# Another hand-written order for a fused attention and channel-mix kernel: other steps of VectorE and GpSimd lie beside each other, and early gaps of TensorE take more zero matmuls

## The chip, the core and the metric

One core of a Trainium2 chip runs the program. The metric is the device time of one launch in microseconds (us). The engines are TensorE (PE in the profile; PEld for its weight loads), VectorE (DVE), ScalarE (ACT), GpSimd (POOL) and SyncE (SP), which issues most of the DMAs. Each engine does its instructions in the order in which the program hands them over; semaphores hold an instruction until its inputs are there and its output buffer is free.

## The reference

Inputs: q, k, v of 4 batches x 4 heads x 1088 positions x 32, two sketches S1, S2 of 8 x 32, and the weights of a channel mix of width 128 with 1024 hidden units.

```python
def phi(x):
    a = np.einsum('rd,bhsd->bhsr', S1, x)
    b = np.einsum('rd,bhsd->bhsr', S2, x)
    return np.einsum('bhsi,bhsj->bhsij', a, b).reshape(*x.shape[:-1], r * r)
q_p, k_p = (phi(q), phi(k))
kv = np.einsum('bhsf,bhsd->bhfd', k_p, v)
z = np.sum(k_p, axis=2)
num = np.einsum('bhsf,bhfd->bhsd', q_p, kv)
den = np.einsum('bhsf,bhf->bhs', q_p, z)[..., None] + 1e-06
x = num / den            # heads side by side: 4 x 1088 x 128
x_prev = x one position earlier, zeros first
xk = mu_k * x + (1.0 - mu_k) * x_prev
xr = mu_r * x + (1.0 - mu_r) * x_prev
k = np.maximum(xk @ w_k, 0.0)
out = 1.0 / (1.0 + np.exp(-(xr @ w_r))) * (k * k @ w_v)
```

## The kernel before

The program is a list of small tasks, written out by hand in a table `ORDER` and carried out in that order; the kernel's last loop looks each name up and calls the function of that name. Nothing else decides the order: an engine's queue is the sequence of the table's entries that use the engine. An entry reads `name.batch.part.engine@banks`. The engine's letter is V (VectorE), A (ScalarE), G (GpSimd) or P (VectorE, with one factor read straight from PSUM); the digits behind @ are PSUM banks that the entry writes.

For each of the 4 batches (first number b):
- `turn.k`, `turn.q` (L259, L262) transpose k and q in 32 x 32 blocks on VectorE; `kproj` (L272, L278) multiplies with the sketches, `abev` (L200) copies the result out of PSUM.
- `kp` (L296) forms phi(k): products of two sketch values, each factor repeated 8 times by a step of zero in its access pattern. The first part of a batch has 1280 elements a partition, the second 1024. `kvmm` (L325), `kvev`, `kvt`, `kvtev` make the summary kv and turn it; `zmm`, `zev`, `wmm`, `wsq` make z and place it in the matrix `SQ`.
- `abw` (matmuls L359, L363, L375, L382) and `abwev` project q; `pw` (L403), `den` (L410, L411) and `an` (L419) form the denominator and scale one factor with it, repeating it; `qp` (L428) forms the scaled phi(q) with repeated factors, parts of 1152 and 1024 elements.
- For batch 0 `qt`/`qtt`, `qtev`/`qttev` transpose qp by TensorE; for the others `qd` (L437) does it on VectorE. `xmm` (L489, L506) and `xt` (L469, L475) give x in PSUM, `xev` and `xtev` copy it to `qx`, `xs` copies the 31 boundary values of a partition to where the shifted x needs them.

Then, for 9 groups g of up to 512 columns (two per batch, the ninth of 256 columns over all batches): `xk`, `xkt` (L522, L525) mix x with its shift, `xh` and `xht` cast x to bf16 (544 or 96 elements), `f1` (L546) multiplies with w_k in four parts, `relu` (L554, ScalarE) empties PSUM, `sq` (L567 on ScalarE, L569 elsewhere) squares, `f2` (L579) multiplies with w_v, `rr` (L592) with w_r, `sig` (L600) is the sigmoid, `fin` (L605) multiplies the two and issues four stores (L612).

`cset`, `smm` and `wset` prepare constants and weights; `wset.0` scales and casts w_k to bf16 (L208, 1024 elements). `zz.n` issues n matmuls of zeros (L173) that nothing reads. Every copy and cast goes through one helper, so L202 stands for all of VectorE's and GpSimd's and L200 for ScalarE's.

```python
def zz(n, banks):
    for i in range(n):
        nc.tensor.matmul(PS[:, banks[0], :], zero[:, :P], zero[:], skip_group_check=True)

def qp(b, g, eng):                                   # L421
    ...
    b_ = pslot(b, g, 0) if eng == "P" else x[:, s0:s1, 0]
    e = nc.gpsimd if eng == "G" else nc.vector
    e.tensor_mul(o[:, :s1 - s0], _ap(a_, list(a_.ap[1:]) + [[0, R]]),
                 _ap(b_, [list(b_.ap[1]), [0, R], list(b_.ap[2])]))

for entry in ORDER.split():                          # L617
    ...
    does[name](*args)
```

Of the kernel before, what the change touches and what calls it, by code (L numbers as in the profile page):

```python
# [35 lines left out]
turn.q.0.1.V kproj.0.1@1 turn.q.0.0.V abev.0.1.A zz.2@7 zmm.0@2 zev.0.V zz.1@7 wmm.0 wsq.0 zz.1@7 abw.0.0@1
abwev.0.0.A kp.0.0.P kp.0.1.G abw.0.1@2 abwev.0.1.A pw.0.0.V den.0.0 an.0.0.G turn.k.1.2.V qp.0.0.P kvmm.0@0 kvev.0.A
pw.0.1.G den.0.1 zz.1@7 kvt.0 zz.1@7 kproj.1.0@3 abev.1.0.A kproj.1.1@4 abev.1.1.A qtt.0@3 qt.0.0@56 qttev.0.A
kvtev.0.V zmm.1@0 zev.1.A an.0.1.G xt.0 qp.0.1.P cset.3 qtev.0.0.A xtev.0.A turn.q.1.2.V qt.0.1@12 wmm.1 wsq.1
wset.0.G qtev.0.1.A xmm.0.0@7 xev.0.0.A xs.0.V xh.0.0.A kp.1.0.G kp.1.1.P xk.0.0 turn.k.2.2.V wset.2.G abw.1.0@0  # L40
abwev.1.0.A abw.1.1@4 abwev.1.1.A pw.1.2.G den.1.2 f1.0.0@12 relu.0.0.A f1.0.3@56 xmm.0.1@4 wset.1.G relu.0.3.A
kproj.2.1@1 an.1.2.V kproj.2.0@5 sq.0.0.A abev.2.1.A sq.0.3.A xev.0.1.V f1.0.1@67 xk.0.1 abev.2.0.V qp.1.0.G qp.1.1.G
xkt.0 turn.k.3.2.V qd.1.0.V relu.0.1.A f1.1.1@01 zmm.2@5 kp.2.0.G zev.2.A sq.0.1.A f1.1.0@23 relu.1.0.A f1.1.2@67
relu.1.2.A wmm.2 wsq.2 kvmm.1@4 kvev.1.A kproj.3.0@5 f1.0.2@23 kproj.3.1@6 turn.q.2.2.V abw.2.0@7 abev.3.0.V
relu.1.1.A qd.1.1.V abev.3.1.A zmm.3@0 turn.q.3.2.V relu.0.2.A zev.3.A abwev.2.0.A abw.2.1@1 abwev.2.1.V sq.1.2.A
kvt.1 wmm.3 wsq.3 kp.2.1.G kvtev.1.A f1.1.3@23 relu.1.3.A abw.3.0@0 abwev.3.0.A kp.3.1.P xt.1@4 kvmm.2@6 xtev.1.A
xht.0.V sq.0.2.V sq.1.3.A kvev.2.A pw.2.2.G den.2.2 xh.0.1.G xmm.1.2@0123 xev.1.0.A an.2.2.G abw.3.1@7 kvt.2 kp.3.0.P
xs.1.G xev.1.1.A qp.2.0.G qp.2.1.G sq.1.0.A abwev.3.1.V xk.1.0 xk.1.1 xh.1.0.V f2.0.0@5 f2.0.1 sq.1.1.A xkt.1 rr.0@7
sig.0.A f2.0.2 f1.3.3@01 f2.0.3 kvtev.2.V pw.3.2.G relu.3.3.A fin.0.S f1.2.2@23 relu.2.2.A rr.1@6 f1.2.3@01 relu.2.3.A
f1.2.0@45 relu.2.0.A sq.3.3.G sig.1.A kvmm.3@2 qd.2.0.V qd.2.1.V f1.3.1@01 kvev.3.V den.3.2 relu.3.1.A rr.2@3 sig.2.A  # L50
xh.1.1.V kvt.3 xmm.2.2@4567 kvtev.3.V xev.2.0.A xt.2@0 xtev.2.V f2.1.0@1 f2.1.1 xs.2.V xev.2.1.V xk.2.0 an.3.2.G xkt.2
sq.2.0.A xh.2.0.A xk.2.1 f1.2.1@23 relu.2.1.A sq.2.3.V f2.1.2 f2.1.3 rr.3@0 sig.3.A f1.3.0@45 relu.3.0.A f1.5.1@67
sq.2.2.V sq.2.1.V f1.3.2@23 relu.3.2.A f2.2.0@0 relu.5.1.A f2.2.1 f2.2.2 sq.3.1.V f1.4.0@45 qp.3.0.G relu.4.0.A
sq.3.0.V f2.3.0@2 f1.4.2@67 relu.4.2.A sq.3.2.V fin.1.S f2.3.1 f1.4.3@34 relu.4.3.A qp.3.1.G f2.2.3 xh.2.1.V f1.5.0@56
relu.5.0.A qd.3.0.V f2.3.2 f1.4.1@34 fin.2.S rr.4@7 qd.3.1.V relu.4.1.A f2.3.3 fin.3.S f1.5.2@01 xmm.3.2@3456 sig.4.A
sq.4.0.V sq.4.2.V sq.5.1.G relu.5.2.A xev.3.1.A sq.4.1.V xev.3.0.V xt.3@7 f1.5.3@01 f2.4.0@2 f2.4.1 f2.4.2 xtev.3.A
xs.3.G xkt.3 rr.5@7 relu.5.3.A xk.3.0 xk.3.1 f1.6.0@01 sq.5.0.V sq.4.3.A f2.4.3 f1.7.1@34 xht.1.G xht.2.G fin.4.S
f2.5.0@5 sq.5.2.V sq.5.3.V sig.5.A relu.6.0.A relu.7.1.A sq.7.1.V f1.6.1@67 relu.6.1.A xht.3.V f2.5.1 f1.6.2@01
sq.6.0.V f1.8.0@23 sq.6.1.V relu.6.2.A relu.8.0.A sq.8.0.V sq.6.2.V f2.5.2 f1.6.3@67 f2.5.3 fin.5.S relu.6.3.A
# [594 lines left out]
```

## Time and profile before

| | |
|---|---|
| time, median of 3 runs | 87.34 us (86.89 to 91.38) |
| the profiled execution | 86.8 us, of which its span 85.0 us |
| busy, share of the span | TensorE 86%, VectorE 81%, ScalarE 70%, GpSimd 46% |
| chain that ended last, by engine | TensorE 31%, VectorE 21%, DMA 19%, issue 19%, GpSimd 2% |
| granted TensorE clock | 0.987 of full speed over the span |
| bytes read and written | 7.80 MB and 2.23 MB |

The span is what the profiler saw between the first and the last instruction; the remaining 1.8 us lie around it. A row of the timeline gives the start in us from the span's start, the duration, the engine, the source line, the operation and its tiles. A row of groups gives count, busy us and the mean ns of one, then the idle time of the engine ahead of them and what ended it.

### The profile page before, as it was taken

The page shows a single profiled execution, that of the slowest core. Times are in us where ns is not written, and L with a number is a line of the kernel's source. Part 1 is how long each engine was busy: PE and PEld are TensorE (multiplying, and loading weights), DVE is VectorE, ACT ScalarE, POOL GpSimd, SP SyncE. Part 2 cuts the span into 40 slices and gives each one's busy share as a digit, 9 for nine tenths or more (in the row PEclk, how much of TensorE's full clock was granted, in tenths as well). Part 3 has the DMA queues.
Part 4 walks back from the last instruction along what each step waited for, and adds up shares of the span by engine and source line. Part 5 has one row for each costly group of instructions (what it writes and reads, how often), then busy time and mean ns, then how long its engine had stood idle before and what let it go on. Part 6 is the DMA issues. An engine that isn't in the chain of part 4 may idle for free.

```text
span 85.0 us, 3444 instructions
## 1 busy us (share of the span) xinstructions
PE 73.0 (86%) x1471; PEld 54.8 (64%) x1483; DVE 69.2 (81%) x121; ACT 59.6 (70%) x88; POOL 39.4 (46%) x53
## 2 busy tenths in 40 slices
PE   4999798998699998999799996999967999999400
PEld 1368696983447667676676784587836877799300
DVE  5367659899979999795889959999998999989600
ACT  0603041468599999994979988799938999999100
POOL 5050904599188999439978199108001700000110
PEclk9999999999999999999999999999999999999995
DMA  0999999999995200000002200001233313042350
GB/s 1 296 314 253 340 384 243 286 400 410 334 217 147 71 12 0 8 0 12 0 8 59 70 2 8 0 0 47 76 93 79 87 27 100 4 121 65 92 142 17
DMA packets 10131, 10.25 MB, mean 121 GB/s; under 512 B 1170, under 2 KB 7540, under 8 KB 10116
## 3 DMA queue, kind: packets, MB, share of 16 engines
q1 hardware_dynamic: 10016, 9.97, 39.9%
q8 instruction: 11, 0.18, 0.8%
q10 hardware_dynamic: 68, 0.03, 0.2%
q14 instruction: 4, 0.03, 0.2%
q0 software_dynamic: 32, 0.03, 0.1%
HBM read 7.80 MB, written 2.23 MB: 118 GB/s over the span
## 4 chain that ended last, share of the span: by engine, by line
PE 31%; DVE 21%; DMA 19%; issue 19%; POOL 2%; SPq 2%; POOLq 1%; ACT 1%; ACTq 0%; DVEq 0%
DMA qx<-in_q_dram 11%; DMA k<-in_k_dram 7%; PE ps L546 6%; DVE k L569 5%; PE ps L382 5%; PE ps L325 4%; DVE qx L202 4%; PE ps L506 3%; DVE qpT L437 3%; PE ps L272 3%; PE ps L579 2%; DVE k L605 2%; DVE x L202 2%; PE ps L592 2%; PE ps L278 2%
## 5 line engine op out<-in xcount | busy, mean ns | idle before, releaser
L554 ACT ACTIVATE k<-ps 128x1024 bf16<-128x1024 f32 (+1 forms) x36 | 33.0, 996 | 2.1 <-DVE k L569 1.5
L579 PE MATMUL ps<-wv,k 128*128 128x128 bf16 x272 | 19.4, 219 | 0.7 <-issue 0.6
L579 PEld LDWEIGHTS <-k 128*128 128x128 bf16 x272 | 16.8, 98 | 4.4 <-issue 0.7
L546 PE MATMUL ps<-xk,wk 128*128 128x512 bf16 x54 | 16.1, 379 | 0.9 <-ACT k L554 0.4
L569 DVE TENSOR_TENSOR k<-k 128x1024 bf16<-128x1024 bf16 (+1 forms) x25 | 14.8, 641 | 0.3 <-ACT k L554 0.2
L428 POOL TENSOR_TENSOR qp<-an,abw 128x1152 f32<-128x1152 f32 (+1 forms) x6 | 12.3, 2070 | 0.6 <-DVE an L419 0.6
L296 POOL TENSOR_TENSOR kp<-ab 128x1024 f32<-128x1024 f32 (+1 forms) x4 | 8.7, 2176 | 1.9 <-ACT ab L200 1.9
L567 ACT ACTIVATE k<-k 128x1024 bf16<-128x1024 bf16 x9 | 9.5, 1070 | 0.0
L546 PEld LDWEIGHTS <-wk 128*128 128x128 bf16 x72 | 6.0, 99 | 3.0 <-issue 0.6
L437 DVE STREAM_TRANSPOSE qpT<-qp 128x1152 f32<-128x1152 f32 (+1 forms) x6 | 7.6, 1285 | 0.0
L272 PEld LDWEIGHTS ps<-SK,kT 128*128 128x128 f32 x54 | 6.3, 192 | 1.3 <-ACT k L554 0.8
L200 ACT COPY ab<-ps 128x256 f32<-128x256 f32 (+1 forms) x6 | 2.4, 394 | 6.6 <-DVE qT L262 3.8
L612 POOL DMA_DIRECT2D out_dram<-rt x1 | 0.7, 709 | 13.0 <-DVE rt L605 13.0
L382 PE MATMUL ps<-SQ,qT 128*32 128x96 f32 x192 | 5.5, 248 | 1.4 <-DVE kp L296 1.0
L173 PE MATMUL ps<-zero 128*128 128x512 bf16 x15 | 5.6, 487 | 1.2 <-DVE warm L155 1.2
L272 PE MATMUL ps<-SK,kT 128*128 128x64 f32 x54 | 6.6, 276 | 0.0
L262 DVE STREAM_TRANSPOSE qT<-qx 128x1088 f32<-128x1088 f32 (+2 forms) x5 | 5.3, 1069 | 1.1 <-DMA qx<-in_q_dram 1.1
L605 DVE TENSOR_TENSOR k<-ps,k 128x512 f32<-128x512 f32 x8 | 5.4, 677 | 0.9 <-ACT k L554 0.4
L200 ACT COPY abw<-ps 128x432 f32<-128x432 f32 (+1 forms) x6 | 3.1, 516 | 4.1 <-PE ps L363 2.8
L569 POOL TENSOR_TENSOR k<-k 128x1024 bf16<-128x1024 bf16 x2 | 3.8, 1892 | 4.8 <-DVE k L569 3.9
L419 POOL TENSOR_TENSOR an<-abw,den 128x272 f32<-128x272 f32 (+2 forms) x4 | 2.2, 559 | 7.8 <-DVE den L411 7.8
L522 DVE SCALAR_TENSOR_TENSOR xk<-ps,rat,qx 128x512 bf16<-128x512 f32 x8 | 5.8, 740 | 0.0
(106 smaller groups left out, 126.3 us busy)
## 6 DMA issues: line engine op xcount, KB each, us to landing
out_dram<-k SPq DMA_DIRECT2D x32, 64.0 KB, 1.7
k<-in_k_dram SPq DMA_DIRECT2D x6, 272.0 KB, 6.6
qx<-in_q_dram SPq DMA_DIRECT2D x6, 272.0 KB, 6.2
v<-in_v_dram SPq DMA_DIRECT2D x8, 144.0 KB, 6.3
v<-in_v_dram SPq DMA_DIRECT2D x8, 128.0 KB, 4.5
wk_f<-in_moe_w_k_dram SPq DMA_DIRECT2D x1, 512.0 KB
wv_f<-in_moe_w_v_dram SPq DMA_DIRECT2D x1, 512.0 KB, 7.7
k<-in_k_dram SPq DMA_DIRECT2D x1, 288.0 KB, 2.8
```

The lines of the kernel that those rows point to most:

```text
L272: nc.tensor.matmul(_ap(o[:, 32 * (m - m0):], [[n, 2], [1, 32]]), kT[b % 2][:].rearrange("p u a -> p (u a)")[:, P * m:P * m + P], SK[:].rea ...
L296: e.tensor_mul(o[:], _ap(a_, list(a_.ap[1:]) + [[0, R]]), _ap(b_, [list(b_.ap[1]), [0, R], list(b_.ap[2])]))
L382: nc.tensor.matmul(d, qT[b % 2][:, 16 * g + (4 * t + c if TURN[b] == "O" else 4 * c + t), :], SQ[b][:].rearrange("p h r -> p (h r)") if TU ...
L428: e.tensor_mul(o[:, :s1 - s0], _ap(a_, list(a_.ap[1:]) + [[0, R]]), _ap(b_, [list(b_.ap[1]), [0, R], list(b_.ap[2])]))
L437: nc.vector.transpose(sb["qpT", b][:].rearrange("p s y a -> p (s y a)")[:, F * s0:F * s1], sb["qp", b, g][:].rearrange("p s i j -> p (s i ...
L522: nc.vector.scalar_tensor_tensor(like(o[:], b), ps["x", b, g], rat[:], like(xslots(b, g, 0), b), op0=MUL, op1=ADD)
L546: nc.tensor.matmul(h[:, c, :], wk[:, 2 * cp + c].rearrange("p y f -> p (y f)"), x, skip_group_check=True)
L554: nc.scalar.activation(o[:, :, :size(g)], h, RELU)
L567: nc.scalar.activation(o[:, :, :n], k1[:, :, :n], SQUARE)
L569: (nc.gpsimd if eng == "G" else nc.vector).tensor_mul(o[:, :, :n], k1[:, :, :n], k1[:, :, :n])
L579: nc.tensor.matmul(o[:, i * P:i * P + P], k2[:, c, i * P:i * P + P], wv[:, 2 * cp + c, :], start=(cp == 0 and c == 0 and i == 0), stop=(cp ...
L605: nc.vector.tensor_mul(o, ps["o", g][:, :n], o)
```

## The change

Only the table `ORDER` is another one; no function is changed. Its first and last lines:

```diff
-turn.k.0.0.V smm.0@0 zz.3@7 smm.1@1 cset.0 cset.4.G turn.k.0.1.V zz.3@7 kproj.0.0@0 abev.0.0.A cset.1.V cset.2.G
+turn.k.0.0.V smm.0@0 cset.0 turn.k.0.1.V zz.4@7 smm.1@1 cset.1.V cset.4.V zz.4@7 kproj.0.0@0 abev.0.0.A cset.2.G
...
-fin.7.S fin.8.SAG
+sig.8.A f2.8.1 f2.8.2 f2.8.3 fin.8.SAG
```

The set of tasks is the same, but for the engines that do them. Zero matmuls in the table go from 12 to 19. Of the squares, GpSimd does 12 instead of 2, VectorE 16 instead of 25 and ScalarE 8 instead of 9. Of the eight `qp`, VectorE does six with both factors in SBUF (V), where it did two with one factor in PSUM (P), and GpSimd two instead of six. Of the eight `kp`, VectorE does two V and one P instead of four P. Of the four `xs`, ScalarE does three and GpSimd one, where VectorE and GpSimd did two each; of the eight `xh`, VectorE does one instead of three and GpSimd six instead of three. `wset.0` goes from GpSimd to VectorE. `fin.6` moves to just ahead of `fin.7`. The loads and their order are the same.

VectorE early, around the first `xk`: the rows name `qp` (phi of q), `qpTt` and `qpTO` (its transposes, copied from PSUM), `qx` (x), `wk` (the scaled weight) and `kp`; + is the changed program.

```order
 L262 STREAM_TRANSPOSE qT_96<-qx_73 128x1088
+L428 TENSOR_TENSOR qp<-an,abw 128x1024
+L202 COPY qpTt<-ps 128x128
+L202 COPY qx_72<-ps 128x64
+L208 TENSOR_SCALAR wk<-wk_f,omu 128x1024
 L316 TENSOR_TENSOR SQ_175<-ps,m_153 128x4x8
-L202 COPY qx_72<-qx_72 128x31
-L296 TENSOR_TENSOR kp_380<-ab_318,ps 128x1024
+L202 COPY qpTO<-ps 128x1024
 L522 SCALAR_TENSOR_TENSOR xk<-ps,rat,qx_72 128x512
```

The second half of batch 0's `qp`, three copies and the scaling of w_k now stand ahead of the first `xk`; the short copy of x and the `kp` of batch 1 have left VectorE.

GpSimd from the `an` and `qp` of batch 1 on (the two rows without a sign), where batches 2 and 3 follow: `k` is a hidden group, its rows L569 are squares, `x` is the bf16 cast of x.

```order
+L202 CAST x_450<-qx_72 128x544
 L419 TENSOR_TENSOR an<-abw,den 128x272
 L428 TENSOR_TENSOR qp<-an,abw 128x1152
-L428 TENSOR_TENSOR qp<-an,abw 128x1024
-L569 TENSOR_TENSOR k_1241<-k_1086 128x1024
-L202 COPY qx_75<-qx_75 128x31
+L296 TENSOR_TENSOR kp_567<-ab_516 128x1280
+L569 TENSOR_TENSOR k_596<-k_452 128x1024
+L296 TENSOR_TENSOR kp_663<-ab_577 128x1280
+L403 TENSOR_TENSOR pw_161<-abw 128x34x8
+L569 TENSOR_TENSOR k_667<-k_527 128x1024
```

Squares now stand between and behind the `kp` of batches 2 and 3, the second part of a `qp` has left GpSimd, and the last square and short copy that it had before are gone from there.

VectorE at the end of the program: L605 is `fin`, `k_71` the buffer in which groups 6 and 7 end, `rt` that of group 8.

```order
+L569 TENSOR_TENSOR k_1473<-k_1471 128x1024
+L569 TENSOR_TENSOR k_1503<-k_1501 128x2x256
+L202 CAST X16T<-qx_72 128x3x32
+L605 TENSOR_TENSOR k_71<-ps,k_71 128x512 x2
 L605 TENSOR_TENSOR rt<-ps,rt 128x256
```

The two `fin` of groups 6 and 7 stand side by side, behind the last squares and a cast of batch 0's x, with `fin.8` behind them.

More of the change, by code (lines that the diff above doesn't have):

```diff
@@ L34 @@
 ORDER = """
-turn.k.0.0.V smm.0@0 zz.3@7 smm.1@1 cset.0 cset.4.G turn.k.0.1.V zz.3@7 kproj.0.0@0 abev.0.0.A cset.1.V cset.2.G
[L36 to L59, printed above, removed]
@@ L60 @@
-sq.6.3.V f1.7.2@01 relu.7.2.A xh.3.0.G f1.7.3@23 f2.6.0@4 f1.7.0@67 relu.7.0.A sq.7.2.V f2.6.1 rr.6@5 sq.7.0.V sig.6.A
-f2.6.2 f1.8.2@01 relu.8.2.A f2.8.0@6 f2.6.3 fin.6.S relu.7.3.A xh.3.1.G f2.7.0@5 f1.8.1@01 f2.7.1 relu.8.1.A sq.7.3.V
-sq.8.1.V f1.8.3@23 rr.7@4 relu.8.3.A f2.7.2 f2.7.3 f2.8.1 rr.8@2 sq.8.3.V sq.8.2.V f2.8.2 f2.8.3 sig.7.A sig.8.A
-fin.7.S fin.8.SAG
+turn.k.0.0.V smm.0@0 cset.0 turn.k.0.1.V zz.4@7 smm.1@1 cset.1.V cset.4.V zz.4@7 kproj.0.0@0 abev.0.0.A cset.2.G
+kproj.0.1@1 kp.0.0.G turn.q.0.1.V turn.q.0.0.V abev.0.1.A zz.3@7 zmm.0@0 kp.0.1.P zev.0.A zz.2@7 wmm.0 wsq.0 zz.2@7
@@ new lines @@
+abw.0.0@1 abwev.0.0.A cset.3 pw.0.0.P abw.0.1@0 kvmm.0@2 kvev.0.A zz.2@7 kvt.0 den.0.0 an.0.0.G turn.k.1.2.V zz.2@7
+kproj.1.1@1 abwev.0.1.A kproj.1.0@3 abev.1.1.A qp.0.0.G pw.0.1.P den.0.1 qtt.0@1 an.0.1.G abev.1.0.A kvtev.0.A
+qt.0.0@45 zmm.1@2 turn.q.1.2.V zev.1.A qtev.0.0.A kp.1.1.G kp.1.0.G qp.0.1.V qttev.0.V xt.0 xtev.0.V xs.0.A wset.0.V
+qt.0.1@67 wmm.1 wsq.1 xmm.0.0@3 xev.0.0.A xh.0.0.A wset.2.G qtev.0.1.V xk.0.0 abw.1.1@2 abwev.1.1.A abw.1.0@6
+abwev.1.0.A xmm.0.1@7 turn.k.2.2.V wset.1.G xev.0.1.A pw.1.2.G den.1.2 f1.0.0@45 xh.0.1.G relu.0.0.A f1.0.2@23
@@ new lines @@
+relu.0.2.A sq.0.2.A kproj.2.0@6 f1.0.3@45 xkt.0 xk.0.1 kproj.2.1@1 abev.2.1.A f1.1.1@23 turn.q.2.2.V kvmm.1@7
+turn.k.3.2.V abev.2.0.A zmm.2@6 relu.0.3.A kvev.1.A kproj.3.0@1 f1.1.0@45 an.1.2.G qp.1.0.G qp.1.1.V zev.2.A qd.1.0.V
+wmm.2 wsq.2 relu.1.1.A kp.2.0.G kvt.1 relu.1.0.A kvtev.1.V f1.0.1@23 abev.3.0.A qd.1.1.V abw.2.1@0 sq.0.0.G relu.0.1.A
+abwev.2.1.A abw.2.0@1 sq.1.1.A xmm.1.2@2345 kp.2.1.V xev.1.1.V kp.3.0.G abwev.2.0.A pw.2.2.G sq.0.3.G kproj.3.1@0
+abev.3.1.A xev.1.0.V xt.1@7 xtev.1.A xs.1.A xkt.1 rr.0@6 xk.1.0 sq.1.0.G sig.0.A f1.1.3@01 relu.1.3.A sq.1.3.G
@@ new lines @@
+kvmm.2@7 zmm.3@6 sq.0.1.A xk.1.1 f1.1.2@01 den.2.2 relu.1.2.A f1.2.1@23 an.2.2.V qp.2.0.V qd.2.0.V f2.0.0@4 f2.0.1
+xh.1.0.G zev.3.V relu.2.1.A f1.2.2@01 relu.2.2.A f2.0.2 kvev.2.V f1.2.0@23 relu.2.0.A sq.1.2.A sq.2.1.G f2.0.3
+sq.2.2.G qp.2.1.V f1.3.0@01 fin.0.S relu.3.0.A wmm.3 f2.1.0@5 f2.1.1 sq.2.0.G kvt.2 kvtev.2.V f1.3.1@23 relu.3.1.A
+f2.1.2 f1.2.3@01 relu.2.3.A wsq.3 qd.2.1.V rr.1@6 sig.1.A f2.1.3 xh.1.1.G f1.3.2@23 rr.2@7 turn.q.3.2.V relu.3.2.A
+xt.2@0 xtev.2.V sig.2.A sq.3.1.A abw.3.1@6 xmm.2.2@1234 xev.2.0.A xev.2.1.A fin.1.S abw.3.0@7 sq.2.3.A sq.3.2.A
@@ new lines @@
+kp.3.1.V xs.2.G xh.2.0.G abwev.3.1.V abwev.3.0.V pw.3.2.G xk.2.0 xkt.2 f2.2.0@5 f2.2.1 f2.2.2 sq.3.0.G f1.3.3@67
+f2.2.3 relu.3.3.A sq.3.3.G xk.2.1 f1.4.0@01 relu.4.0.A den.3.2 an.3.2.V sq.4.0.G f1.5.1@23 rr.3@4 sig.3.A f1.4.2@67
+relu.4.2.A sq.4.2.G fin.2.S rr.4@5 sig.4.A f1.4.3@01 relu.5.1.A qp.3.0.V kvmm.3@4 kvev.3.A relu.4.3.A f1.4.1@67
+relu.4.1.A f2.3.0@5 f2.3.1 f2.3.2 f2.3.3 qp.3.1.V kvt.3 kvtev.3.A qd.3.0.V qd.3.1.V fin.3.S sq.4.3.V sq.4.1.V
+f1.5.0@23 f1.5.2@01 relu.5.0.A xh.2.1.G relu.5.2.A xmm.3.2@4567 xev.3.1.V xt.3@2 xtev.3.A xs.3.A xkt.3 f2.4.0@3
@@ new lines @@
+f1.5.3@01 relu.5.3.A f2.4.1 f2.4.2 rr.5@2 xev.3.0.V xk.3.0 xk.3.1 f1.6.1@01 f2.4.3 sig.5.A sq.5.1.G relu.6.1.A
+sq.5.0.V f1.6.2@45 relu.6.2.A f1.6.0@67 xht.2.G relu.6.0.A fin.4.S sq.5.2.V f2.5.0@2 f1.6.3@01 sq.5.3.V xht.1.G f2.5.1
+f1.7.0@34 sq.6.1.V xh.3.0.V f2.5.2 sq.6.0.V f1.8.0@56 xh.3.1.G f2.5.3 fin.5.S rr.6@7 relu.6.3.A sq.6.2.V xht.3.V
+relu.7.0.A sq.7.0.V relu.8.0.A sq.8.0.V sig.6.A f2.6.0@0 f1.8.1@34 relu.8.1.A f1.7.2@12 relu.7.2.A sq.6.3.V f2.6.1
+f1.7.1@56 relu.7.1.A sq.7.2.V sq.7.1.V f2.6.2 f1.7.3@34 sq.8.1.V f1.8.3@12 f2.6.3 relu.7.3.A sq.7.3.V f2.7.0@7 rr.7@5
@@ L64 @@
+f2.7.1 f1.8.2@34 relu.8.3.A sq.8.3.V sig.7.A f2.7.2 xht.0.V f2.8.0@1 f2.7.3 relu.8.2.A rr.8@3 sq.8.2.A fin.6.S fin.7.S
+sig.8.A f2.8.1 f2.8.2 f2.8.3 fin.8.SAG
 """
```

## The prediction

> **What bounds the kernel now.** I read the page's busy shares first, then the busy time by stretches, the chain that ended last, and the timeline at the places where VectorE (DVE) is slow.
>
> ```profile
> PE 73.0 (86%) x1471; PEld 54.8 (64%) x1483; DVE 69.2 (81%) x121; ACT 59.6 (70%) x88; POOL 39.4 (46%) x53
> ```
> ```profile
> 24.00:40.00 16.00, 15.29 (x518) 11.22 (x517) 14.48 (x22) 14.73 (x24) 12.73 (x11) 1.00 0.22 53
> 40.00:48.00 8.00, 7.34 (x166) 5.66 (x158) 6.95 (x11) 7.46 (x11) 5.96 (x4) 1.00 0.13 34
> 48.00:54.00 6.00, 5.18 (x128) 4.04 (x126) 4.95 (x11) 4.84 (x8) 4.81 (x3) 1.00 0.03 6
> 54.00:63.00 9.00, 8.25 (x105) 5.91 (x121) 9.00 (x12) 8.33 (x10) 1.89 (x1) 1.00 0.15 40
> 63.00:80.00 17.00, 16.05 (x276) 13.29 (x249) 15.58 (x29) 14.88 (x21) 1.85 (x5) 1.00 0.28 74
> ```
> The columns are the stretch, its length, and the busy us of PE, PEld, DVE, ACT and POOL. From 24 us on three engines are about 90% busy at once, and the granted clock (1.00) leaves nothing for more filler to win. DVE idles 1.52, 1.05, 1.05 and 0 us in the first four stretches, 3.6 in all. POOL idles 7.1 of 9 us in the fourth and 15 of 17 in the last.
>
> ```profile
> 50.43 1.82 DVE qx L202 x2
> ...
> 53.76 3.61 DVE k L569 x6
> ...
> 57.97 1.65 DVE x L202
> ...
> 61.48 1.15 DVE qpT L437
> ```
> These are pieces of the chain that ended last. From 50.2 to 63.8 us it runs on DVE alone, so there every microsecond of DVE counts. Two pieces are far too long for their work:
>
> ```profile
> 18.43 2.39 POOL L296 TENSOR_TENSOR kp<-ab 128x1280 f32<-128x1280 f32 x1
> 19.69 1.17 DVE L202 COPY qx<-qx 128x31 f32<-128x31 f32 x1
> ...
> 42.44 1.01 DVE L202 CAST x<-qx 128x544 bf16<-128x544 f32 x1
> ...
> 49.45 4.09 POOL L428 TENSOR_TENSOR qp<-an,abw 128x1152 f32<-128x1152 f32 x2
> 50.43 1.23 DVE L202 COPY qx<-qx 128x31 f32<-128x31 f32 x1
> ...
> 57.43 1.89 POOL L569 TENSOR_TENSOR k<-k 128x1024 bf16<-128x1024 bf16 x1 [3.89 <-DVE k L569]
> 57.90 1.72 DVE L202 CAST x<-qx 128x544 bf16<-128x544 f32 x1
> ...
> 48.48 0.38 DVE L202 CAST x<-qx 128x544 bf16<-128x544 f32 x1
> 38.88 0.21 POOL L202 COPY qx<-qx 128x31 f32<-128x31 f32 x1
> ```
> A 31-element copy takes 1.17 us and ends at 20.86, just after POOL's kp ends at 20.82; the cast at 57.90 ends 0.30 us after POOL's square. The same cast, started while POOL was free (48.48), takes 0.38. So such a DVE step stands still until POOL's running instruction ends. Over their free durations (0.2 for the copy, as POOL's own row of it says, 0.38 for the cast) the four lose 0.97, 0.63, 1.03 and 1.34, that is 4.0 us.
>
> ```profile
> 16.31 2.14 POOL L208 TENSOR_SCALAR wk<-wk_f,omu 128x1024 bf16<-128x1024 f32 x1
> ...
> 17.69 0.78 DVE L224 TENSOR_TENSOR rat<-tmp,mu 128x1 f32<-128x1 f32 x1
> ```
> One product does so too: `rat`, one element, both factors in SBUF, ends with POOL's wk (18.45), 0.6 us lost.
>
> **The change part by part.** The rows for the sums:
>
> ```profile
> L569 DVE TENSOR_TENSOR k<-k 128x1024 bf16<-128x1024 bf16 x21 | 13.4, 683 | 0.2 <-ACT k L554 0.2
> L428 DVE TENSOR_TENSOR qp<-an,ps 128x1152 f32<-128x1152 f32 x1 | 1.3, 1316 | 0.0
> L428 DVE TENSOR_TENSOR qp<-an,ps 128x1024 f32<-128x1024 f32 x1 | 1.2, 1222 | 0.4 <-POOL an L419 0.4
> L296 DVE TENSOR_TENSOR kp<-ab,ps 128x1280 f32<-128x1280 f32 x2 | 2.9, 1452 | 0.0
> L428 POOL TENSOR_TENSOR qp<-an,abw 128x1152 f32<-128x1152 f32 x3 | 6.5, 2179 | 0.6 <-DVE an L419 0.6
> L569 POOL TENSOR_TENSOR k<-k 128x1024 bf16<-128x1024 bf16 x2 | 3.8, 1892 | 4.8 <-DVE k L569 3.9 <-ACT k L554 0.9
> L262 DVE STREAM_TRANSPOSE qT<-qx 128x1088 f32<-128x1088 f32 x3 | 3.9, 1285 | 0.0
> L554 ACT ACTIVATE k<-ps 128x1024 bf16<-128x1024 f32 x32 | 31.1, 1044 | 2.1 <-DVE k L569 1.5 <-PE ps L592 0.3
> ```
> *POOL* takes ten more squares (10 x 1.89 = 18.9 us), two more kp of 1280 (4.8) and three more casts (1.9); it loses four of its six qp (8.1), the wk scale (2.1), a kp of 1024 and small things (about 4). It ends near 51 us of work instead of 39.4.
>
> *DVE in the middle*, from xmm.0.1 to xmm.3.2 (24 to 63 us before). In come five qp (2 x 1.32 + 3 x 1.22 = 6.3), a kp (1.2), a turn (1.3) and small steps that stood elsewhere (den, an, zev, together 1.5): 10.3 us. Out go five squares (3.4), a kp of 1280 (1.45), three casts and the short copy at their free durations (1.3), two abev (0.9) and an xht (0.25): 7.3. So DVE's own work grows by 3.0, and the waits at 42.44, 50.43 and 57.90 (0.63 + 1.03 + 1.34 = 3.0) go. These cancel. What can still be won there is DVE's 3.6 us of idle time, if its work no longer slips behind POOL: between 0 and -3.6. I take -1.5, a little under half, since PE and ACT are about as full and stand next in line.
>
> *DVE and ACT at the end*, after xmm.3.2: ACT sheds a relu (1.04), a sig and an xev and gets a short copy (2.1 us less), DVE sheds four squares, one of half size (2.5), and gets an xev, a cast and an xht (1.2 us less in all). Between 0 and -2.1; I take -1.2, since DVE is the fuller of the two (15.58 of 17 us).
>
> *The early part* loses the copy's 0.97 and pays for fillers and a new order:
>
> ```profile
> 3.68 1.13 PE L173 MATMUL ps<-zero 128*128 128x512 bf16 x3
> 5.27 0.82 PE L173 MATMUL ps<-zero 128*128 128x512 bf16 x3
> 10.12 2.03 PE L363 MATMUL ps<-SQ,qT 128*128 128x96 f32 x16
> 12.07 1.21 PE L325 MATMUL ps<-kp,v 128*32 128x64 f32 x72
> 12.18 0.48 ACT L200 COPY abw<-ps 128x384 f32<-128x384 f32 x1 [0.37 <-DVE pw L403]
> 17.80 1.02 ACT L200 COPY qpTO<-ps 128x1024 f32<-128x1024 f32 x1
> 22.84 1.04 PE L546 MATMUL ps<-xk,wk 128*128 128x512 bf16 x3
> 23.81 1.06 PE L489 MATMUL ps<-qpTO,kvt 64*32 64x512 f32 x8
> ```
> Seven more zero matmuls: those of the first group start 0.35 us apart (three from 3.68 to 4.73), later ones 0.22. Two stand ahead of kproj.0.0, which waited for no input in its last 0.4 us: +0.6. One each ahead of zmm.0, wmm.0 and abw.0.0 is partly hidden by abev and zev: in all abw.0 is 0.8 later (its row at 10.12 moves to 10.9) and kvmm.0 behind it (12.07) too. ACT now does kvev.0 ahead of the second abw copy, which slips from 12.18 to about 14.4; den.0.1 ends at 15.9 as before, because DVE no longer does qp.0.0 there. POOL does qp.0.0 (14.05 to 16.2) and an.0.1 behind it; qp.0.1 starts at 17.1, the first qpTO copy at 19.0 instead of 17.80, xmm.0.0 at 20.4; the second copy (DVE) ends at 21.6 and xk.0.0 starts at 22.0, hardly later than before, where the short copy at 19.69 and a kp of batch 1 had held it. f1.0.0 then comes at 23.8 instead of 22.84, but xmm.0.1 has been done ahead of it; at 24.7 both programs have done the same matmuls. That is 0 if the wk scale, now a DVE step, meets no kp of POOL. POOL runs two kp back to back there, to 21.1, and the scale is ready at 19.5: if it stands still like a cast, what is queued behind it on DVE (wsq.1, the second qpTO copy, xk.0.0) and with these abw.1, xmm.0.1 and f1.0.0 are 1.0 later. No row shows that step on DVE; its own price lies between a cast's 0.38 and POOL's 2.14, and I take 0.65, near the cast. For the early part I take +0.3 of 0 to +1.0.
>
> *The tail.*
>
> ```profile
> 78.80 0.69 DVE L605 TENSOR_TENSOR k<-ps,k 128x512 f32<-128x512 f32 x1
> ...
> 79.52 1.77 SPq L612 DMA_DIRECT2D out_dram<-k  x4
> ...
> 81.81 0.80 SPq L612 DMA_DIRECT2D out_dram<-rt  x2
> ```
> fin.6 moves from 76.09 to just ahead of fin.7, behind sq.8.3 and an xht. SP then has ten stores to issue in a row at about 0.45 us, not six: fin.7's four queue behind fin.6's four. Counted from fin.7's start, SP's last issue ended after 3.8 us; ten issues counted from fin.6, 0.6 us ahead of fin.7, end after 0.7 + 4.6 - 0.6 = 4.7. Between 0 (fin.6 ready early) and +0.9, I take +0.6.
>
> **Sum:** +0.3 - 1.5 - 1.2 + 0.6 = -1.8. The profiled execution took 86.8 us (span 85.0, 1.8 around it), 0.5 under the median of 87.34, so 85.0.
>
> **The rivals.** *Products stand still too (B).* All of this supposes that the DVE products with a repeated factor (kp, qp, an) run beside POOL. Before, DVE's kp and qp took one factor from PSUM; now six qp and two kp take both from SBUF, as `rat` does. For: `rat`'s row, the only such product beside a busy POOL. Against: it repeats no factor, and no row shows one that does. The price: of these eight and two an, nine lie in the middle, where POOL is busy about 0.85 of the time (51 us of work in some 60) with instructions of about 2 us, so half of one on average: 9 x 0.85 x 1.0 = 7.7 us on a DVE with 3.6 us of idle, of which I let 2 absorb it; net +5.5, so 90.5, slower. Behind each waiting product stands a qd or an abwev on DVE, and behind that an xmm on PE. It decides from about 0.4 us of waiting for each product, which uses up the 1.8 gained and the 2 of slack.
>
> The Trainium skill, "SBUF — State Buffer", section "Who interferes with whom", says that a DVE instruction with two SBUF inputs contends with a GpSimd instruction that reads SBUF and that the later one blocks fully. The traces bear it out at `rat` (0.78 us); it excepts no repeated factor, and by it this rival would hold.
>
> *The plan doesn't close the gaps (C).* Products run free, but the scale meets kp (early +1.0), and ten squares at 1.89 instead of 0.68 us make POOL as full as DVE, so the idle stays (0): 1.0 - 1.2 + 0.6 = +0.4, 87.2. For it speaks that the own work of DVE doesn't fall.
>
> **How the numbers follow.** Forecast (A) 85.0, chance 0.47, its own range 83.2 to 86.6; B 90.5 (87.5 to 92), 0.38; C 87.2, 0.15. About 2% is what a measurement here tells from no change. Faster by over 2%, that is under 85.6 against the median: two thirds of A and a little of C and B, 0.36; within 2%: a third of A, most of C and a tenth of B, 0.31; slower: 0.33. The range reaches from 83.2 to 91.0: some 0.06 lies below, 0.13 above.
>
> **What would show it.** Short copies at 0.2 us and casts at 0.4 beside a busy POOL, or on other engines. DVE's qp (L428) at 1.2 to 1.3 us in A, at 2 us and more in B. POOL near 51 us, with squares at 1.9. The first f1 near 23.8 us, the last xmm near 61 in A, past 65 in B. SP's last ten stores without a gap. I am wrong if a PSUM bank taken earlier holds PE in the middle, which I have not followed step by step.

## The result, and the profile after

The changed kernel took 96.4 and 96.65 us, against 86.89 and 87.34 before: 1.108 times as long, with an interval of 1.094 to 1.122. It is slower, where 85.0 was forecast. (In about half of the executions of most kernels here TensorE's matmuls take nearly twice as long up to 14 to 21 us after the start, 3.94 instead of 2.12 us for the first 18 of `kproj`, which adds 2 to 6 us; times below leave these late executions out unless they are called so, and of a late profile only stretches that begin behind that point are compared.) The profiled execution of the changed kernel took 96.65 us, its span 94.8, 9.8 more than before.

The busy times by engine, and then by the same kind of stretches as before (columns: stretch, length, busy us of PE, PEld, DVE, ACT and POOL, granted clock, DMA share, GB/s):

```profile
PE 77.3 (82%) x1490; PEld 56.1 (59%) x1490; DVE 78.1 (82%) x119; ACT 58.0 (61%) x88; POOL 59.4 (63%) x55
```
```profile
40.00:48.00 8.00, 6.52 (x142) 4.45 (x140) 7.86 (x10) 7.63 (x11) 8.00 (x6) 1.00 0.01 3
48.00:54.00 6.00, 5.23 (x49) 4.07 (x50) 6.00 (x9) 2.83 (x4) 6.00 (x3) 0.72 0.17 44
54.00:63.00 9.00, 8.68 (x222) 6.24 (x220) 6.69 (x14) 8.47 (x13) 5.30 (x7) 1.00 0.12 33
63.00:72.00 9.00, 6.89 (x170) 4.85 (x181) 9.00 (x6) 6.74 (x9) 9.00 (x5) 1.00 0.13 33
```

DVE is busy 8.9 us longer than before and POOL 20.0. In three of the four stretches both are full at once (48:54 and 63:72 wholly). PE, which had been the fullest over the span, idles 1.5 us of 40:48 and 2.1 us of 63:72, and in 48:54 its granted clock is 0.72. The chain that ended last has moved with it: DVE's share went from 21% to 35%, and `qp` (L428) alone has 12% of the span.

```profile
DVE 35%; DMA 24%; issue 19%; PE 10%; SPq 4%; POOLq 1%; POOL 1%; DVEq 0%
```

The groups of instructions by form (count, busy us, mean ns) show what "busy" means here:

```profile
L428 DVE TENSOR_TENSOR qp<-an,abw 128x1024 f32<-128x1024 f32 x4 | 10.9, 2724 | 0.0
L428 DVE TENSOR_TENSOR qp<-an,abw 128x1152 f32<-128x1152 f32 x2 | 5.4, 2686 | 0.0
L296 DVE TENSOR_TENSOR kp<-ab 128x1024 f32<-128x1024 f32 x2 | 3.6, 1822 | 0.0
L569 POOL TENSOR_TENSOR k<-k 128x1024 bf16<-128x1024 bf16 x12 | 26.9, 2260 | 0.0
L296 POOL TENSOR_TENSOR kp<-ab 128x1280 f32<-128x1280 f32 x4 | 10.6, 2648 | 1.2 <-ACT ab L200 1.2
```

The smaller qp takes 2.72 us as a mean, although it has fewer elements than the other (2.69): the length isn't work. With one factor in PSUM the same products took 1.32, 1.22 and (kp) 1.22 us. The eight DVE products with both factors in SBUF are 10.9 + 5.4 + 3.6 = 19.9 us long where their own work is 2 x 1.32 + 6 x 1.22 = 10.0: **9.9 us of standing still**, 1.24 each in the mean. (One of them, the kp at 56.31, met an idle POOL and took its own 1.22.) The two `an` on DVE took 0.89 us in the mean instead of 0.44. POOL's squares and kp are longer too, 2.26 and 2.65 us where the rows of before had 1.89 and 2.40.

The timeline at one place, DVE first, then POOL, then PE:

```profile
43.16 1.10 DVE L419 TENSOR_TENSOR an<-abw,den 128x272 f32<-128x272 f32 x1
44.30 2.93 DVE L428 TENSOR_TENSOR qp<-an,abw 128x1152 f32<-128x1152 f32 x1
47.26 1.38 DVE L437 STREAM_TRANSPOSE qpT<-qp 128x1152 f32<-128x1152 f32 x1
48.56 0.15 DVE L202 COPY zs<-ps 128x32 f32<-128x32 f32 x1
```
```profile
40.23 5.79 POOL L569 TENSOR_TENSOR k<-k 128x1024 bf16<-128x1024 bf16 x3
45.96 1.76 POOL L202 CAST x<-qx 128x544 bf16<-128x544 f32 x1
```
```profile
46.27 0.59 PE L546 MATMUL ps<-xk,wk 128*128 128x512 bf16 x2
48.77 0.41 PE L313 MATMUL ps<-zs,ZL 128*128 128x32 f32 x2 [1.91 <-DVE zs L202]
...
50.33 1.06 PE L546 MATMUL ps<-xk,wk 128*128 128x512 bf16 x2
...
53.99 0.59 PE L546 MATMUL ps<-xk,wk 128*128 128x512 bf16 x2
```

The qp at 44.30 ends at 47.23, 1.2 us behind POOL's third square (46.02), which is nearly its own length: it did nothing before. POOL's cast, queued behind that square, takes 1.76 us (0.64 at 27.40) and ends 0.5 us behind the qp: now POOL stood still. Behind the qp on DVE stand its transpose and the 0.15 us copy of z, and PE waits 1.91 us for that copy. The lull has a second price: the same pair of matmuls takes 0.59 us at 46.27, 1.06 at 50.33 and 0.59 again at 53.99, and the granted clock of 48:54 is 0.72.

Early, the first f1 comes at 26.61 instead of 22.84 (DVE, then POOL, then PE):

```profile
17.21 2.96 DVE L428 TENSOR_TENSOR qp<-an,abw 128x1024 f32<-128x1024 f32 x1
...
20.95 2.43 DVE L208 TENSOR_SCALAR wk<-wk_f,omu 128x1024 bf16<-128x1024 f32 x1
```
```profile
17.14 5.30 POOL L296 TENSOR_TENSOR kp<-ab 128x1024 f32<-128x1024 f32 x2
```
```profile
11.28 2.02 PE L363 MATMUL ps<-SQ,qT 128*128 128x96 f32 x16
...
20.43 0.32 PE L469 MATMUL ps<-qpTt,kvt 64*32 64x64 f32 x8 [1.59 <-DVE qpTt L202]
...
23.54 0.87 PE L382 MATMUL ps<-SQ,qT 128*32 128x96 f32 x32 [0.63 <-DVE SQ L316]
...
26.61 1.04 PE L546 MATMUL ps<-xk,wk 128*128 128x512 bf16 x4
```

The last xmm stands in the summary of line L506 (min, median and max ns, then first and last start), before and then after. Behind it the end of the program on DVE and in SP's queue, after, and fin.8 before:

```profile
L506 PE MATMUL ps<-qpT,kvt x192: 371/377/403, 38.2 to 63.9; 32*32 32x256 f32 x192
```
```profile
L506 PE MATMUL ps<-qpT,kvt x192: 371/377/402, 37.5 to 72.3; 32*32 32x256 f32 x192
```
```profile
86.72 1.51 DVE L605 TENSOR_TENSOR k<-ps,k 128x512 f32<-128x512 f32 x2
88.47 0.42 DVE L605 TENSOR_TENSOR rt<-ps,rt 128x256 f32<-128x256 f32 x1 [0.24 <-PE ps L579]
```
```profile
77.84 13.35 SPq L612 DMA_DIRECT2D out_dram<-k  x16
91.71 0.80 SPq L612 DMA_DIRECT2D out_dram<-rt  x2
```
```profile
79.70 0.42 DVE L605 TENSOR_TENSOR rt<-ps,rt 128x256 f32<-128x256 f32 x1 [0.20 <-PE ps L579]
```

With these rows the 9.8 us divide by the prediction's own terms. The last column is the first experiment on the whole kernel below, without the eight products:

| stretch | forecast | before | changed | difference | without the eight products |
|---|---|---|---|---|---|
| start to first f1 | +0.3 | 22.8 | 26.6 | +3.8 | 25.0 (+2.2) |
| first f1 to last xmm | -1.5 | 41.1 | 45.7 | +4.6 | 38.4 (-2.7) |
| last xmm to fin.8 | -1.2 | 15.8 | 16.2 | +0.4 | 16.5 (+0.7) |
| fin.8 to the end of the span | +0.6 | 5.3 | 6.3 | +1.0 | 6.4 (+1.1) |
| sum | -1.8 | 85.0 | 94.8 | +9.8 | 86.3 (+1.3) |

### The profile page after: what moved, and what is told of

Read it like the earlier page. It is cut to its first block, busy times and chain, and to the rows that moved or that the text cites. A ratio compares the mean times of both kernels' runs of the same rounds, so it can differ in the third digit from the quotient of the medians.

```text
span 94.8 us, 3465 instructions
## 1 busy us (share of the span) xinstructions
PE 77.3 (82%) x1490; PEld 56.1 (59%) x1490; DVE 78.1 (82%) x119; ACT 58.0 (61%) x88; POOL 59.4 (63%) x55
## 4 chain that ended last, share of the span: by engine, by line
DVE 35%; DMA 24%; issue 19%; PE 10%; SPq 4%; POOLq 1%; POOL 1%; DVEq 0%
DVE qp L428 12%; DMA wk_f<-in_moe_w_k_dram 8%; DMA qx<-in_q_dram 6%; DMA k<-in_k_dram 6%; DMA v<-in_v_dram 5%; SPq L137 4%; DVE qpT L437 4%; DVE xk L522 4%; DVE k L569 2%; PE ps L579 2%; PE ps L546 2%; DVE qx L202 2%; DVE an L419 2%; DVE kp L296 2%; PE ps L382 2%
## 5 line engine op out<-in xcount | busy, mean ns | idle before, releaser
L569 POOL TENSOR_TENSOR k<-k 128x1024 bf16<-128x1024 bf16 x12 | 26.9, 2260 | 0.0
L546 PE MATMUL ps<-xk,wk 128*128 128x512 bf16 x64 | 19.2, 396 | 0.9 <-DVE xk L522 0.8
L428 DVE TENSOR_TENSOR qp<-an,abw 128x1024 f32<-128x1024 f32 (+1 forms) x6 | 16.2, 2712 | 0.0
L296 POOL TENSOR_TENSOR kp<-ab 128x1280 f32<-128x1280 f32 (+1 forms) x5 | 12.5, 2510 | 1.2 <-ACT ab L200 1.2
L569 DVE TENSOR_TENSOR k<-k 128x1024 bf16<-128x1024 bf16 (+1 forms) x16 | 10.6, 709 | 0.2 <-ACT k L554 0.2
L200 ACT COPY ab<-ps 128x320 f32<-128x320 f32 (+1 forms) x8 | 3.1, 397 | 8.3 <-PE ps L272 7.3
L567 ACT ACTIVATE k<-k 128x1024 bf16<-128x1024 bf16 (+1 forms) x8 | 7.9, 1007 | 0.1
L202 POOL CAST x<-qx 128x544 bf16<-128x544 f32 x6 | 4.9, 824 | 4.1 <-issue 2.3
L506 PE MATMUL ps<-qpT,kvt 32*32 32x256 f32 x192 | 5.0, 385 | 2.1 <-DVE qpT L437 2.1
L382 PEld LDWEIGHTS ps<-SQ,qT 128*32 128x32 f32 x192 | 4.0, 110 | 3.5 <-DVE SQ L316 3.4
```

The source lines that it names most:

```text
L296: e.tensor_mul(o[:], _ap(a_, list(a_.ap[1:]) + [[0, R]]), _ap(b_, [list(b_.ap[1]), [0, R], list(b_.ap[2])]))
L382: nc.tensor.matmul(d, qT[b % 2][:, 16 * g + (4 * t + c if TURN[b] == "O" else 4 * c + t), :], SQ[b][:].rearrange("p h r -> p (h r)") if TU ...
L546: nc.tensor.matmul(h[:, c, :], wk[:, 2 * cp + c].rearrange("p y f -> p (y f)"), x, skip_group_check=True)
L567: nc.scalar.activation(o[:, :, :n], k1[:, :, :n], SQUARE)
L569: (nc.gpsimd if eng == "G" else nc.vector).tensor_mul(o[:, :, :n], k1[:, :, :n], k1[:, :, :n])
```

## The experiments

The theory (X in the expectations): every DVE step that reads two SBUF operands, and every copy, cast or scaling from SBUF to SBUF, shuts GpSimd's SBUF steps out and is shut out by them for whole instructions, whether a factor is repeated or not. The rivals: a repeated factor runs free (F), and the loss is GpSimd's load of squares (S) or the fillers and the early order (Z).

**Single steps (pairs).** This kernel computes nothing of the reference. It has each kind of DVE step alone, behind a POOL product, behind a POOL square, and three of them ahead of one.

```diff
+for with_pool in (None, p_qp, p_sq):
+    for d in (qp, qp with a PSUM factor, plain product, square, short copy, cast, scale, transpose, fin):
+        ...
+        if with_pool: with_pool()
+        pre(); d(); pre()
```

> No attention here: single VectorE steps, each with the sizes of this kernel, once with GpSimd idle, once 0.5 us behind the start of a GpSimd product of 1152 elements (2.2 us) and once behind a GpSimd square (1.9 us); then three of them with VectorE first. Its output is left out but for a corner. Theory X (every VectorE step that reads two SBUF operands or copies SBUF to SBUF excludes GpSimd, a repeated factor or not): the product with repeated factors (L428 in the kernel, 1.32 us alone) lasts until GpSimd's instruction ends and then its full time, 2.8 to 3.1 us; the plain product likewise 2.8 to 3.1, the square 2.0 to 2.6, the short copy 1.4 to 1.9, the cast 1.6 to 2.1, the scale 2.0 to 3; with a factor in PSUM 1.3, transpose 1.3, fin 0.7 unchanged; with VectorE's product first, GpSimd's product takes 3 us instead of 2.2. Theory F (a repeated factor frees the product, as the prediction had it): 1.3 us beside GpSimd, the rest as in X. Theory N (no step waits long; the kernel's long rows came from something else): all within 0.2 us of their time alone.

The timeline of DVE (L146 qp, L149 qp with a PSUM factor, L152 a product without repeats), alone up to 25 us and behind POOL's product from 33 us, then a transpose there; then POOL's product:

```profile
17.63 1.35 DVE L146 TENSOR_TENSOR qp<-an,abw 128x1152 f32<-128x1152 f32 x1
...
22.05 1.35 DVE L152 TENSOR_TENSOR f_o<-f_a,f_b 128x1152 f32<-128x1152 f32 x1
...
33.85 1.90 DVE L146 TENSOR_TENSOR qp<-an,abw 128x1152 f32<-128x1152 f32 x1
...
36.61 1.34 DVE L149 TENSOR_TENSOR qp<-an,ps 128x1152 f32<-128x1152 f32 x1
...
38.82 2.66 DVE L152 TENSOR_TENSOR f_o<-f_a,f_b 128x1152 f32<-128x1152 f32 x1
...
52.84 1.30 DVE L167 STREAM_TRANSPOSE f_o<-f_a 128x1088 f32<-128x1088 f32 x1
...
79.09 1.35 DVE L146 TENSOR_TENSOR qp<-an,abw 128x1152 f32<-128x1152 f32 x1
```
```profile
32.35 2.18 POOL L173 TENSOR_TENSOR qp_g<-an_g,abw_g 128x1152 f32<-128x1152 f32 x1 [31.91 <-ACT an_g L188]
...
79.13 3.34 POOL L173 TENSOR_TENSOR qp_g<-an_g,abw_g 128x1152 f32<-128x1152 f32 x1 [0.63 <-ACT an_g L188]
```

The qp at 33.85 waits for POOL's end at 34.53 and needs 1.22 more; behind a POOL square it took 2.59. Ahead of POOL's product it takes its own 1.35, and POOL's goes from 2.18 to 3.34. The product without repeats is held in the same way (2.66), so F is false. With a PSUM factor (1.34), as a transpose (1.30) or as fin (0.68) a step takes the same with and without POOL. Behind POOL's product the square went from 0.68 to 1.72, the short copy from 0.17 to 1.21, the cast from 0.43 to 1.86 and the scale from 1.12 to 2.25. X is shown, and it works in both directions (the scale held POOL up too: a product that POOL started at 51.35, while the scale ran, took 2.67). That a copy or a cast holds POOL up isn't shown here.

**The eight products taken out of the changed kernel (a_free).**

```diff
 def kp(b, j, eng):
+    if eng == "V":
+        nc.vector.transpose(o, kin[b][:, :F * n])
+        return
 def qp(b, g, eng):
+    if eng == "V":
+        nc.vector.transpose(o[:, :n], src[:, :n])
+        return
```

> The changed program with the eight VectorE products of two SBUF factors (two kp, six qp) left out and VectorE transposes of the same count of elements from one loaded SBUF tile put in their place (1.2 to 1.35 us each). Theory X: their waits go (in the changed program's trace the six qp take 2.71 us in the mean instead of 1.27, the squares of GpSimd 2.26 instead of 1.89), 6 to 10 us of the 9.8 come back: 87 to 91 us against 96.5. Rival Z (the fillers and the early order cost it): 94 to 96. Rival S (ten squares at 1.9 us on GpSimd make GpSimd the bound): 93 to 96, with GpSimd busy without a gap in the middle.

This kernel leaves phi out in these eight places. It took 88.02, 87.97 and 87.4 us, against 86.16 and 87.28 of the kernel before beside it (ratio 1.011, interval 0.980 to 1.043; 87.5 and 88.11 were measured too and aren't in the ratio). So 8.4 to 9.2 us of the changed kernel's time go with the standing still of eight instructions and what follows from it; their own DVE time is still there as transposes. The transposes read a loaded tile and so wait for no input; but the eight products had no idle time ahead of them either (0.0 in their rows), so little can come from that. POOL keeps all its twelve squares, and they and its kp are short again:

```profile
L577 POOL TENSOR_TENSOR k<-k 128x1024 bf16<-128x1024 bf16 x12 | 23.3, 1960 | 0.0
L299 POOL TENSOR_TENSOR kp<-ab 128x1280 f32<-128x1280 f32 x4 | 9.6, 2403 | 1.4 <-ACT ab L200 1.4
```
```profile
L208 DVE TENSOR_SCALAR wk<-wk_f,omu 128x1024 bf16<-128x1024 f32 x1 | 3.1, 3095 | 0.0
```

POOL's busy time falls from 59.4 to 52.4 us with the same instructions: 7 us of it had been waiting. POOL is full over whole stretches here too, and PE is nearly full beside it, so S is false:

```profile
40.00:48.00 8.00, 7.87 (x92) 5.88 (x91) 7.93 (x12) 7.62 (x9) 8.00 (x6) 1.00 0.05 13
54.00:63.00 9.00, 8.69 (x186) 6.11 (x187) 8.93 (x12) 8.58 (x13) 9.00 (x6) 1.00 0.13 33
```

What remains is in the early part, at the end and in the tail (the table's last column). Early, the scale of w_k, still behind POOL's kp, takes 3.1 us.

**Three products moved the same way in the kernel before (b_prod).**

```diff
-qp.1.1.G ... qp.2.1.G ... qp.3.1.G
+qp.1.1.V ... qp.2.1.V ... qp.3.1.V
```

> The program before with one part of the change alone: qp.1.1, qp.2.1 and qp.3.1 on VectorE with both factors in SBUF, not on GpSimd. They start together with GpSimd's qp of the first part. Theory X: each waits about 2 us for it on VectorE, L428 rows of 2.5 to 3.3 us, time +2 to +5 us (89 to 92). Theory F: rows of 1.25 us, GpSimd 5.9 us lighter, time 86 to 87, no more than 0.5 above before.

The one execution that wasn't late took 90.45 us, 3.2 to 4.3 over the kernel before. In the profile, a late one, the stretch from the first xk to fin.8 (27.5 to 88.7) is 61.2 us, against 57.8 before (21.9 to 79.7): +3.4. The three products:

```profile
L428 DVE TENSOR_TENSOR qp<-an,abw x3: 1577/2503/2919, 33.0 to 65.7; 128x1024 f32<-128x1024 f32 x3
```

Their sum is 7.0 us, 3.3 more than their own 3 x 1.22. Nothing but three letters differs from the kernel before, so neither the order nor the fillers are needed for the standing still: about 1.1 us a product. The time alone doesn't tell this from the 3.7 us of own work that DVE gets here and POOL loses; the rows do, and a_free, which keeps the work and drops the waits.

**The fillers: taken out of the changed kernel (a_zz), put into the kernel before (b_zz), and taken out where the products are gone (a_free_zz).**

```diff
 (a_zz, a_free_zz; b_zz the other way round)
-zz.4@7 ... zz.4@7 ... zz.3@7 ... zz.2@7 ... zz.2@7 ... zz.2@7 ... zz.2@7
+zz.3@7 ... zz.3@7 ... zz.2@7 ... zz.1@7 ... zz.1@7 ... zz.1@7 ... zz.1@7
```

> The changed kernel with the zero matmuls of the kernel before (12 instead of 19 in the table); all else as changed. The first f1 of the changed kernel came 3.8 us later than before (26.61 against 22.84), where +0.3 was forecast. If the fillers are the cause (Z), the seven matmuls less give back 1 to 2 us at the first f1 and in the whole, so 94.5 to 95.5 us. If the cause is DVE products and the scale standing still behind GpSimd (X: qp 2.96 instead of 1.22 at 17.21, the scale 2.43 at 20.95), the first f1 moves by less than 0.8 us and the time stays at 96.0 to 96.7.

> The kernel before with the zero matmuls of the changed one (19 instead of 12 in the table), nothing else. Z: +0.8 us at abw.0 and +0.6 to +1.5 us in the whole, so 87.5 to 88.5. X: what the fillers delay is caught up where DVE and GpSimd hold the order, less than 0.5 us in the whole, 86.9 to 87.5.

> The changed kernel without the eight DVE products that have both factors in SBUF (transposes of the same size in their place, so phi is left out there), and with the zero matmuls of the kernel before. Without these products alone it was 87.4 to 88.0. What is left of the change is then its order, its GpSimd load (some 55 us) and its own tail. Z: 86.0 to 86.9, since the fillers cost about 1 us once nothing else holds the early part. X alone: 87.2 to 88.0, no different.

a_zz took 95.89 us in its one execution that wasn't late, 0.5 to 0.8 under the changed kernel, 0.1 under the least that X gave (96.0) and 0.4 over the most that Z gave (95.5); from its first f1 on (31.7 to 94.3) it isn't faster than the changed kernel (26.6 to 88.5): 62.6 and 61.9 us. All four executions of a_free_zz were late (93.3 to 93.7), so its early part says nothing; from the first f1 on it takes 54.7 us against 54.9 with the fillers, no gain. But b_zz took 89.25 and 89.4, 1.032 times as long as the kernel before (1.024 to 1.039), more than either theory gave: its first f1 comes at 23.6, 0.8 later, and the rest, 1.6 us more up to fin.8, comes far behind the fillers. PE's waits between 30 and 45 us, in b_zz and before:

```profile
PE ps L382 <- issue: 1.8, 2, 1.0
```
```profile
PE ps L382 <- issue: 0.4, 1, 0.4
```

In the middle of abw's matmuls PE waits for nothing that the profile shows, 1.8 us instead of 0.4; in b_prod, b_apart, b_best and b_best5, with 12 zero matmuls, it is at most 0.7. With seven more ahead of it this gap is longer; why, the runs don't show, and the changed kernel, which has the same 19, has no such gap at these matmuls. So fillers have a price in this program; in the changed one, by the one execution of a_zz, it is at most 0.8 of the 9.8 us.

**The blocked copies and casts taken off VectorE, with nothing else (b_apart, b_best, b_best5, b_best2).** These leave the kernel before as it is and move only the four steps that the prediction had found standing still.

```diff
-xs.0.V ... xh.1.0.V ... xs.2.V ... xh.2.1.V
+xs.0.A ... xh.1.0.G ... xs.2.A ... xh.2.1.G
 (b_best and b_best5: xh.2.1.G stands behind sq.5.1.G instead)
 (b_best2: also qp.3.0.G right behind an.3.2.G, and qd.3.0.V ahead of sq.2.3.V)
```

> The program before with the other part alone: the two short copies xs.0 and xs.2 on ScalarE and the casts xh.1.0 and xh.2.1 on GpSimd, so that no copy or cast of VectorE from SBUF stands beside a busy GpSimd. Theory X: 4.0 us of waiting leave VectorE, 2.3 of them inside the stretch where the chain is VectorE alone: 84 to 85.5 us. Rival (the waits were covered by what else is late there): 86.5 to 87.5, the same as before.

> The kernel before with the four short copies and casts taken away from VectorE (copies of batch 0 and 2 to ScalarE, two casts to GpSimd), as one run has had it (-1.5 us between the same two rows, though its squares then waited at 55.86 and 57.30), and here with the second cast of batch 2 behind GpSimd's square of group 5, so that no DVE square meets it. X: that square takes 0.7 instead of 1.1 us and the last product ends 0.3 to 0.8 us earlier than in that run, 2 us before the kernel before: 84.8 to 85.5 with TensorE's clock released as early as there. If what a DVE step loses behind GpSimd isn't what sets the time in this stretch, no different from the kernel before, 86.9 to 87.4.

> The kernel before with its four blocked short copies and casts taken away from VectorE, a second time and in more rounds, because TensorE ran at half speed up to 19.71 us in the profile of the first time. From wsq.1 on it took 1.8 us less than the kernel before. X: where TensorE is released as early as in the kernel before, 84.6 to 85.4 us, 1.5 to 2 us under it. If the waits of these four steps were covered by other work anyway, 86.3 to 87.3.

> The same, and the one DVE square that still waits for GpSimd (1.52 instead of 0.68 us, 58.01, beside qp of batch 3) let go behind a transpose: qd.3.0 stands ahead of it now, which takes no two SBUF operands and runs beside qp.3.1 at its own 1.3 us. X: the square takes 0.7 us and the transpose 1.35, so DVE's stretch up to the last xmm is 0.5 to 0.8 us shorter than without this edit; 84.0 to 84.8 with an early release. If a transpose stands still too, or if PE now waits for the later squares, no gain or a loss of up to 0.5.

b_apart and b_best met only late executions (89.2 to 91.8 and 90.5 to 91.2), so by stretches: from the first wsq behind the late clock (wsq.1) to fin.8 the kernel before took 60.1 us (19.6 to 79.7), b_apart 58.5 (23.7 to 82.2), b_best 58.4 (25.57 to 83.94). The second cast's place gave at most 0.2, less than the 0.3 to 0.8 expected. b_best5 is b_best again, and three of its executions weren't late: 84.47, 85.17 and 85.24 us, against 86.48 to 87.12: **0.978 times the time of the kernel before, interval 0.968 to 0.988**, 1.9 us in the mean; 84.6 to 85.4 us had been expected. The four steps' own 1.2 us (two copies of 0.2, two casts of 0.38) left DVE as well, so a part of it can be that work and not their waiting. In its profile (85.24 us) the short copy that stood between the copies of x and the first of these xk for 1.23 us is gone from DVE, and the squares behind show the one wait that was left, for POOL's last qp:

```profile
49.63 0.97 DVE L202 COPY qx<-ps 128x64 f32<-128x64 f32 x2 [0.98 <-PE ps L475]
50.51 0.74 DVE L522 SCALAR_TENSOR_TENSOR xk<-ps,rat,qx 128x512 bf16<-128x512 f32 x1
...
52.02 4.55 DVE L569 TENSOR_TENSOR k<-k 128x1024 bf16<-128x1024 bf16 x6
```

Six squares in 4.55 us, where before they took 3.68. b_best2 lets a transpose go first (the profile is of a late execution):

```profile
57.57 1.37 DVE L437 STREAM_TRANSPOSE qpT<-qp 128x1152 f32<-128x1152 f32 x1
58.86 3.66 DVE L569 TENSOR_TENSOR k<-k 128x1024 bf16<-128x1024 bf16 x6
62.44 0.68 DVE L605 TENSOR_TENSOR k<-ps,k 128x512 f32<-128x512 f32 x1
64.51 0.69 DVE L605 TENSOR_TENSOR k<-ps,k 128x512 f32<-128x512 f32 x1 [1.39 <-PE ps L579]
```

The edit did what it should: the transpose beside POOL's qp takes its own 1.37, the six squares 3.66. The time didn't move: 85.07, 85.41 and 85.56 (ratio to before 0.982, 0.974 to 0.990), where 84.0 to 84.8 was expected. The squares, which PE needs for `f2`, now stand behind the transpose: counted from the end of the same xk they end after 4.95 us (57.57 to 62.52) instead of 4.55 (52.02 to 56.57), and fin.2, which waits 1.39 us for PE, starts after 6.94 instead of 6.54. The 0.9 us saved are paid for by 1.37 us of other work ahead of what PE waits for; the expectation had named this case.

## Why the prediction was wrong

**The step that failed** is the premise of forecast A, "that the DVE products with a repeated factor (kp, qp, an) run beside POOL". Eight of them were to cost 10.0 us of DVE and cost 19.9, and the whole took 8.4 to 9.2 us longer than without them. The premise was held at 0.47 against B's 0.38 although the only row that bore on it, `rat` at 0.78 us, spoke against it, for the reason that `rat` repeats no factor. The pairs show that this difference counts for nothing. The Trainium skill, "SBUF — State Buffer", section "Who interferes with whom", states the rule without an exception for repeats; the rule holds here (1.90, 2.59 and 2.66 us instead of 1.35), and by it B was the likelier case.

**B had the mechanism, and in the middle nearly the size.** Its middle was -1.5 + 5.5 = +4.0 (7.7 less 2 is 5.7; 5.5 was written) and measured +4.6. The nine steps that it priced at 7.7 us lost about 9.1 there: the seven kp and qp 8.2, the two `an` 0.9. It counted only DVE's wait; POOL's own, some 7 us, and the clock that PE's lull cost came on top. What lies between its 90.5 and 96.65 is for the most part elsewhere: 3.5 us early, 1.6 at the end and 0.4 in the tail, where it kept A's terms. It gave the early part no product at all, where qp.0.1 alone lost 1.74.

**Early, +0.3 against +3.8.** abw.0 moved from 10.12 to 11.28, 1.2 us where 0.8 was taken. The seven zero matmuls alone moved it by 0.8 (10.88 in b_zz); the first matmuls of this execution were also slow, the four zero matmuls at 3.68 taking 1.89 us where the same four took 1.30 in a_free. qp.0.1 was to start at 17.1 and did (17.21), but ended at 20.17 and not at 18.3; PE waited 1.59 us for its transpose. The scale was taken at 0.65, "near the cast", out of 0.38 to 2.14: its own time is 1.12 and behind POOL's kp it was 2.43, above the range. The +1.0 that the prediction set beside this case was about right: PE waited 0.63 and 0.26 us for what stood behind it. Together, 1.2 + 1.6 + 0.9, these make up the 3.8 but for 0.1.

**The middle, -1.5 against +4.6.** Without the eight products it is -2.7: the freed copies and casts, the idle time of DVE and the twelve squares of POOL did what the forecast said, within its 0 to -3.6 (that kernel has transposes in their place, so the size is not to be trusted to tenths).

**The end, -1.2 against +0.4**, and +0.7 without the products. This term was wrong by itself. It reckoned with DVE and ACT, but the quoted row of 63:80 has PE busy 16.05 of 17 us, and the same groups of PE's matmuls stand behind the last xmm in both programs. PE is busy 15.15 of this stretch's 15.8 us before and 15.28 of 16.2 after, where it waits 0.8 us for an xk of DVE. That PE sets this stretch is read from these rows and from b_best5, whose last stretch is as long as before; no run tested it by itself.

**The tail, +0.6 against +1.0.** The mechanism was right: fin.6 and fin.7 stand together at 86.72, and SP ends its stores 4.0 us behind fin.8's start (88.47 to 92.51) instead of 2.9 (79.70 to 82.61). The ten issues were reckoned to end 5.3 us behind fin.6's start (0.7 + 4.6) and ended 5.8 behind it (86.72 to 92.51). The 0.5 us is a pause in SP's queue ahead of the last two issues (91.19 to 91.71), which stood there before too (81.29 to 81.81).

So A would have missed without the blocking too: the kernel without the eight products took 87.4 to 88.0 us, outside A's own 83.2 to 86.6. C's 87.2 is near that, but by luck: it had 0 for the middle and -1.2 for the end, where this kernel shows -2.7 and +0.7.

Of the things to look for: POOL was to be near 51 us and is 59.4, 52.4 without the blocking; DVE's qp (L428) is at 2.7, the sign of B; the last xmm is at 72.3, past 65.
